# A new order for all engines, V of step 2 loaded earlier, and a third output tile in a fused attention and rational-MLP kernel

## The chip, the cores and the metric

The kernel runs on one core of a Trainium2 chip. The metric is the device time of one execution in microseconds (us); before the change the median of three runs is 232.0 us (231.14 to 232.74). Five engines work side by side, each through its own queue and strictly in the order written for it: TensorE (PE in the profile, its weight loads PEld), VectorE (DVE), ScalarE (ACT), GpSimd (POOL) and SyncE (SP). An instruction that waits on another engine or on a DMA holds up all that stands behind it in its own queue.

## The reference, cut to what matters

```python
# q, k, v: (4 batches, 8 heads, 768 positions, 64), float32
scores = q @ k.T / sqrt(64)
keep   = (pos_k < 4) | ((pos_q - pos_k >= 0) & (pos_q - pos_k < 128))   # 4 sink keys, window of 128
attn   = softmax(where(keep, scores, -1e9)) @ v
x      = attn.transpose(0, 2, 1, 3).reshape(3072, 512)
h      = x @ w_in                                   # 512 -> 2048
P      = a0 + a1*h + a2*h**2 + a3*h**3
Q      = 1 + |b0|*|h| + |b1|*h**2
out    = (P / (Q + 1e-6)) @ w_out                   # 2048 -> 512
```

## The kernel before, in words

The 3072 tokens are worked on in 12 steps of 256 tokens, three to a batch. A step s has an attention part and an MLP part; the attention runs some steps ahead of the MLP.

Attention of a step: K and Q are brought into the layout with the head dimension on the partitions. For the first four steps TensorE transposes them (`turn_k0`, `turn_q0`, `turn_kc`, `turn_qc`, line 661), and DVE or ACT copies the result out of PSUM (`place_k0`, `place_kc`, `place_qc`, the helper lines 677 on ACT and 679 on DVE). For later steps SyncE does it by a transposing DMA (lines 711, 715). V of the first three steps is loaded as rows (`load_vc`, line 474), sorted by TensorE (`turn_vc`, line 494) and placed (`place_vc`); later V goes straight to its place (`load_v`, line 465). `scores` (lines 761, 772, 786) come in four groups of a step, `exps` (ACT, line 805) takes the exponential, `attend` (line 846) multiplies by V, `rec` and `norm` (DVE, lines 854, 860) divide, `turn_x` (lines 880, 885) and `placed_x` give the transposed x of the MLP. The four sink keys of V are spread over the partitions by `cast_vs`, `turn_vs` and `spread_vs` (lines 533, 541, 555), in part 0 (batch 0) and part 1 (batches 1 to 3); `split_ab` (line 627) and `turn_vs:0` bring the coefficients a and b, which `norm` needs too.

MLP of a step m: `gemm1:m,j` (line 910, j from 0 to 3) multiplies by a quarter of w_in, `copy_in` (ACT, line 917) takes it out of PSUM, `sqa` (ACT) or `sqd` (DVE) squares it, `and`, `den`, `even`, `odd`, `odd_h`, `num`, `gate` (DVE, lines 930 to 964) are the rational function, `ln` and `exp` (ACT, lines 954, 959) the reciprocal of its denominator. `gemm2` (line 974) multiplies by w_out, `copy_out` and `store` bring out the rows. Steps 0 and 11 are cut into four parts for the elementwise work.

GpSimd issues the loads of w_in, w_out, V, K and Q (`load_kc` 440, `load_qc` 449, `load_k` 458, `load_q` 427, `load_w_in` 511, `load_w_out` 517), and holds some of them back by a one-element copy (`hold`, line 507) that waits for x_n or hb of a step.

Everything is cut into some 820 pieces. Each piece names its engine, its planned length, what it comes after, and, on TensorE, which of four PSUM tiles (`ps_h`, `ps_o`, `ps_m`, `ps_s`) it takes and which piece frees it. The list ORDER of numbers is the order in which the pieces are emitted, and so every engine's order; it comes from a search made ahead of time, and no planner runs in the kernel. ENGINE says for 32 copies whether DVE or ACT does them, BANK which PSUM tile each TensorE piece takes. A TensorE piece can start only when the piece that frees the last user of its tile is done. A negative number in ORDER is a stretch of idle matmuls (`spin`).

Of the kernel before, what the change touches and what calls it, by code (L numbers as in the profile page):

```python
# [65 lines left out]
def kernel(  # L66
# [54 lines left out]
    ENGINE = {('cast_q0', 1): 'DVE',  # L121
               ('place_kc', 3, None): 'DVE',
               ('place_qc', 0, 0): 'ACT',
               ('place_qc', 0, 1): 'ACT',
               ('k_sink', 0): 'DVE',
               ('place_qc', 1, None): 'DVE',
               ('place_qc', 2, None): 'DVE',
               ('place_qc', 3, 0): 'ACT',
               ('place_vc', 0): 'DVE',
               ('placed_x', 0, 0): 'ACT',  # L130
               ('placed_x', 0, 1): 'DVE',
# [8 lines left out]
               ('place_vc', 2): 'ACT',  # L140
               ('cast_k0', 0): 'DVE',
               ('place_k0', 0): 'DVE',
               ('cast_k0', 1): 'DVE',
               ('place_k0', 1): 'ACT',
               ('cast_q0', 0): 'ACT',
               ('place_kc', 1, None): 'ACT',
               ('place_kc', 2, None): 'ACT',
               ('place_qc', 3, 1): 'ACT',
               ('k_sink', 1): 'ACT',
# [23 lines left out]
             ('attend', 10, 0): 'ps_s',
             ('attend', 10, 1): 'ps_o',
             ('attend', 11, 0): 'ps_o',
             ('attend', 11, 1): 'ps_s',
             ('gemm1', 0, 0): 'ps_o',
             ('gemm1', 0, 1): 'ps_s',
             ('gemm1', 0, 2): 'ps_m',
             ('gemm1', 0, 3): 'ps_o',  # L180
             ('gemm1', 1, 0): 'ps_s',
             ('gemm1', 1, 1): 'ps_o',
# [14 lines left out]
             ('gemm1', 5, 0): 'ps_s',
             ('gemm1', 5, 1): 'ps_m',
             ('gemm1', 5, 2): 'ps_o',
             ('gemm1', 5, 3): 'ps_h',  # L200
# [13 lines left out]
             ('gemm1', 9, 1): 'ps_h',
             ('gemm1', 9, 2): 'ps_o',
             ('gemm1', 9, 3): 'ps_m',
             ('gemm1', 10, 0): 'ps_h',
# [1212 lines left out]
```

## Time and profile before

| | |
|---|---|
| median of 3 runs | 232.0 us (231.14 to 232.74) |
| the profiled execution: its time, its span | 232.42 us, 230.7 us |
| busy: TensorE, VectorE, ScalarE, GpSimd | 215.9, 211.1, 207.0, 97.3 us |
| granted TensorE clock over the span | 1.00 |

The profiled execution lies 0.4 us above the median; its time is 1.7 us longer than the span from its first to its last instruction. Three engines are busy for 90 to 94% of the span. In the slices of the page the idle part lies in the first 60 us and in the last 6.

### The profile page before, as it was taken

How to read it: one execution, taken by the hardware profiler on the slowest of the kernel's cores; microseconds unless marked ns; L12 is line 12 of the kernel's file. 1: busy time of each engine (PE TensorE's matmuls, PEld its weight loads, DVE VectorE, ACT ScalarE, POOL GpSimd, SP SyncE). 2: the span in 40 equal slices, each digit the busy share in tenths (PEclk: the TensorE clock that was granted, in tenths of full speed). 3: DMA queues.
4: the chain of work that ended last, by engine and by line, in shares of the span. 5: the costliest groups of instructions: out<-in, count | busy, mean ns of one | idle time of the engine just before them, and what ended most of it. 6: DMA issues, size and time to landing. Idle time of an engine off the chain costs nothing.

```text
span 230.7 us, 7350 instructions
## 1 busy us (share of the span) xinstructions
PE 215.9 (94%) x3249; PEld 147.0 (64%) x3271; DVE 211.1 (91%) x251; ACT 207.0 (90%) x177; POOL 97.3 (42%) x126
## 2 busy tenths in 40 slices
PE   8768999989999999999999999999999999999992
PEld 2546777778747667667677577758856875544441
DVE  3595699879999999999999999999999999999991
ACT  2757889989997999999999999999999999799961
POOL 8914756967559499988199800000000000000000
PEclk9999999999999999999999999999999999999999
DMA  6999999999999999999969998230050200400152
GB/s 182 199 191 199 197 144 103 135 117 121 205 176 141 130 106 150 172 122 124 196 155 133 109 148 162 47 71 0 3 139 3 48 0 0 182 4 0 49 224 91
DMA packets 95237, 26.98 MB, mean 117 GB/s; under 512 B 85862, under 2 KB 92262, under 8 KB 95206
## 3 DMA queue, kind: packets, MB, share of 16 engines
q0 software_dynamic: 65024, 12.98, 90.4%
q1 hardware_dynamic: 28942, 12.75, 29.8%
q10 hardware_dynamic: 1240, 0.79, 1.1%
q8 instruction: 25, 0.41, 0.8%
q14 instruction: 6, 0.05, 0.1%
HBM read 27.30 MB, written 6.29 MB: 146 GB/s over the span
## 4 chain that ended last, share of the span: by engine, by line
PE 69%; DMA 19%; POOL 3%; DVE 3%; issue 2%; ACT 2%; SPq 0%; DVEq 0%; ACTq 0%
PE ps_s L974 13%; PE ps_h L974 11%; PE ps_o L910 9%; PE ps_m L974 9%; PE ps_m L910 7%; DMA w_out_sb<-in_moe_w_out_dram 6%; PE ps_s L910 5%; PE ps_h L910 5%; DMA stage_v<-in_v_dram 4%; DMA k_bf<-in_k_dram 3%; DMA stage_a<-in_k_dram 2%; POOL v L465 2%; DMA ab_row<-in_moe_a_dram 2%; PE ps_o L846 2%; DMA q_bf<-in_q_dram 1%
## 5 line engine op out<-in xcount | busy, mean ns | idle before, releaser
L910 PEld LDWEIGHTS <-w_in_sb 128*128 128x128 bf16 x768 | 73.8, 98 | 13.0 <-issue 1.2
L974 PEld LDWEIGHTS <-g 128*128 128x128 bf16 x386 | 36.4, 98 | 41.6 <-issue 1.4
L954 ACT ACTIVATE lnq<-den 128x4096 f32<-128x4096 bf16 (+3 forms) x18 | 44.6, 2482 | 1.5 <-DVE den L935 1.4
L959 ACT ACTIVATE den<-lnq 128x4096 bf16<-128x4096 f32 (+3 forms) x18 | 44.5, 2484 | 0.2
L465 POOL DMA_DIRECT2D v<-in_v_dram x48 | 35.0, 746 | 3.6 <-DMA w_out_sb<-in_moe_w_out_dram 1.5
L910 PE MATMUL ps_o<-xblk,w_in_sb 128*128 128x256 bf16 x304 | 36.3, 273 | 0.0
L974 PE MATMUL ps_s<-w_out_sb,g 128*128 128x512 bf16 x136 | 32.3, 379 | 0.8 <-issue 0.5
L974 PE MATMUL ps_h<-w_out_sb,g 128*128 128x512 bf16 x121 | 28.6, 379 | 0.9 <-issue 0.5
L964 DVE TENSOR_TENSOR g<-num,den 128x4096 bf16<-128x4096 bf16 (+3 forms) x18 | 28.3, 1572 | 0.3
L935 DVE TENSOR_TENSOR den<-den,sq 128x4096 bf16<-128x4096 bf16 (+3 forms) x18 | 28.3, 1570 | 0.2
L951 DVE TENSOR_TENSOR num<-num,sq 128x4096 bf16<-128x4096 bf16 (+3 forms) x18 | 28.3, 1572 | 0.1
L948 DVE TENSOR_TENSOR sq<-sq,hb 128x4096 bf16<-128x4096 bf16 (+3 forms) x18 | 28.2, 1569 | 0.1
L910 PE MATMUL ps_m<-xblk,w_in_sb 128*128 128x256 bf16 x208 | 24.9, 273 | 0.5 <-DMA w_in_sb<-in_moe_w_in_dram 0.5
L974 PE MATMUL ps_m<-w_out_sb,g 128*128 128x512 bf16 x90 | 21.6, 379 | 0.6 <-issue 0.5
L917 ACT ACTIVATE hb<-ps_o 128x1024 bf16<-128x1024 f32 x19 | 19.5, 1029 | 2.1 <-PE ps_o L910 1.9
L924 ACT ACTIVATE sq<-hb 128x1024 bf16<-128x1024 bf16 (+3 forms) x15 | 20.0, 1341 | 0.1
L427 POOL DMA_DIRECT2D q_bf<-in_q_dram x15 | 16.7, 1111 | 6.0 <-DMA w_out_sb<-in_moe_w_out_dram 2.6
L910 PE MATMUL ps_s<-xblk,w_in_sb 128*128 128x256 bf16 x160 | 19.1, 273 | 0.0
L940 DVE TENSOR_SCALAR num<-sq,acoef 128x4096 bf16<-128x4096 bf16 (+3 forms) x18 | 18.3, 1023 | 0.3
L944 DVE TENSOR_SCALAR sq<-sq,acoef 128x4096 bf16<-128x4096 bf16 (+3 forms) x18 | 18.4, 1021 | 0.3
L507 POOL COPY seen<-x_n 1x1 bf16<-1x1 bf16 x8 | 9.7, 1225 | 17.4 <-DVE x_n L860 17.4
L926 DVE TENSOR_TENSOR sq<-hb 128x2048 bf16<-128x2048 bf16 (+2 forms) x13 | 16.8, 1295 | 0.1
(154 smaller groups left out, 321.5 us busy)
## 6 DMA issues: line engine op xcount, KB each, us to landing
out_dram<-o_t SPq DMA_DIRECT2D x11, 512.0 KB, 3.6
w_in_sb<-in_moe_w_in_dram POOLq DMA_DIRECT2D x4, 512.0 KB, 10.8
k_bf<-in_k_dram POOLq DMA_DIRECT2D x16, 128.0 KB, 6.6
w_out_sb<-in_moe_w_out_dram POOLq DMA_DIRECT2D x4, 512.0 KB, 11.7
q_bf<-in_q_dram POOLq DMA_DIRECT2D x15, 128.0 KB, 5.4
v<-in_v_dram POOLq DMA_DIRECT2D x24, 64.0 KB, 6.3
stage_v<-in_v_dram POOLq DMA_DIRECT2D x3, 256.0 KB, 9.6
v<-in_v_dram POOLq DMA_DIRECT2D x24, 32.0 KB, 5.7
```

The lines of the kernel that those rows point to most:

```text
L465: nc.gpsimd.dma_start(out=v_fix[b % 2][half(r), g * NHF:(g + steps) * NHF, hl, 0:D], in_=v[b, h, g * TS:(g + steps) * TS, :].rearrange("(j ...
L910: nc.tensor.matmul(ps[:, n, :], lhsT=w_in_all[:, c, fc * P:(fc + 1) * P], rhs=xblk[m][:, c, :], start=(c == 0), stop=(c == NDMC - 1))
L917: nc.scalar.activation(out=hb[m][:, j * GW:(j + 1) * GW], in_=ps_h.pop((m, j)).rearrange("p n c -> p (n c)"), func=AF.Copy)
L924: nc.scalar.activation(out=sq[m][:, c], in_=hb[m][:, c], func=AF.Square)
L935: nc.vector.tensor_tensor(out=den[m][:, c], in0=den[m][:, c], in1=sq[m][:, c], op=ALU.add)
L944: nc.vector.tensor_scalar(out=sq[m][:, c], in0=sq[m][:, c], scalar1=a3, scalar2=a1, op0=ALU.mult, op1=ALU.add)
L948: nc.vector.tensor_tensor(out=sq[m][:, c], in0=sq[m][:, c], in1=hb[m][:, c], op=ALU.mult)
L951: nc.vector.tensor_tensor(out=num[m][:, c], in0=num[m][:, c], in1=sq[m][:, c], op=ALU.add)
L954: nc.scalar.activation(out=lnq_fix[:, c], in_=den[m][:, c], func=AF.Ln, scale=qsc_reg, bias=1.000001)
L959: nc.scalar.activation(out=den[m][:, c], in_=lnq_fix[:, c], func=AF.Exp, scale=-1.0)
L964: nc.vector.tensor_tensor(out=g_of[m][:, c], in0=num[m][:, c], in1=den[m][:, c], op=ALU.mult)
L974: nc.tensor.matmul(ps_out[own][:, tt, cols], lhsT=g_of[m][:, co:co + P], rhs=w_out_all[:, fc, cols], start=(fc == 0), stop=(fc == NFFC - 1 ...
```

## The change

- ORDER is another permutation, ENGINE changes side for 20 of its 32 copies, BANK for most of the TensorE pieces.
- The first spin is 14 wide and 2 narrow matmuls in place of 13 and 2, and the second spin (5 matmuls, in step 0's attention) is gone.
- The pool of output tiles has three buffers, and `copy_out` of step m comes after `store` of step m-3 in place of m-2. To make room, the small tile `stage_s` (sink rows of V) becomes a slice of `stage_b`, which holds the first Q.
- `load_vc:2` moves on GpSimd's queue to the place right behind the first quarter of w_in.
- Nothing is computed in another way.

```diff
 ORDER = [
-    118, 2, 3, 0, -154, 108, 107, 129, 109, 117, 4, 119, 113, 116, 120, 121, 122, 1, 125, 143,
+    118, 2, 3, 0, -358, 108, 107, 109, 14, 119, 113, 120, 121, 122, 1, 116, 125, 5, 15, 8, 146,
...
-    ENGINE = {('cast_q0', 1): 'DVE',
-               ('place_kc', 3, None): 'DVE',
+    ENGINE = {('cast_q0', 1): 'ACT',
+               ('place_kc', 3, None): 'ACT',
...
-             ('scores', 0, 0): 'ps_h',
-             ('scores', 0, 1): 'ps_s',
+             ('scores', 0, 0): 'ps_o',
+             ('scores', 0, 1): 'ps_m',
...
-    o_sb = ctx.enter_context(tc.tile_pool(name="o_sb", bufs=2))
+    o_sb = ctx.enter_context(tc.tile_pool(name="o_sb", bufs=3))
...
-    stage_s = const_pool.tile([SR, B, D], FP32, name="stage_s")
+    stage_s = stage_b[0:SR, NQ0 * H * D:NQ0 * H * D + B * D].rearrange("p (b d) -> p b d", b=B)
...
-                      ends + [("store", m - 2, 0) if m >= 2 else None],
+                      ends + [("store", m - 3, 0) if m >= 3 else None],
...
-          [("gemm2", LAST, 1, parts(LAST) - 1), ("store", LAST - 2, 0)])
+          [("gemm2", LAST, 1, parts(LAST) - 1), ("store", LAST - 3, 0)])
```

Three places in the engines' queues follow, each first as it was and then as it is. Place one: GpSimd's loads around w_in (511 is w_in, 474 V rows of a step, 440 K rows, 449 Q rows, 458 K of later steps, 427 Q of later steps, 465 V of later steps). Before:

```order
L511 DMA w_in_sb<-in_moe_w_in_dram 128x4x512
L449 DMA stage_d<-in_q_dram 128x8x64
L511 DMA w_in_sb<-in_moe_w_in_dram 128x4x512 x2
L507 COPY seen<-x_n 1x1
L465 DMA v_92<-in_v_dram 64x4x64
L440 DMA stage_v<-in_k_dram 128x8x128
L511 DMA w_in_sb<-in_moe_w_in_dram 128x4x512
L474 DMA stage_v<-in_v_dram 128x8x128
```

Now:

```order
L449 DMA stage_d<-in_q_dram 128x8x64
L511 DMA w_in_sb<-in_moe_w_in_dram 128x4x512
L474 DMA stage_v<-in_v_dram 128x8x128
L511 DMA w_in_sb<-in_moe_w_in_dram 128x4x512 x2
L458 DMA k_bf<-in_k_dram 128x8x64
L511 DMA w_in_sb<-in_moe_w_in_dram 128x4x512
L427 DMA q_bf<-in_q_dram 128x8x64
L440 DMA stage_v<-in_k_dram 128x8x128
```

V of step 2 (474) has moved ahead of three quarters of w_in, K of step 3 (440) behind all four, and no hold copy stands among them.

Place two: DVE from `split_ab` on (627), with `spread_vs` (555, and 553 for the coefficients) in step 0's attention. Before:

```order
L627 TENSOR_TENSOR ab_part<-ab_row 1x8
L533 CAST sink_rows<-stage_s 32x192
L679 CAST v_91<-ps_o 128x16x64
L553 COPY ab_bc<-ps_m 128x8
L555 TENSOR_TENSOR v_sink<-ps_m,ind 128x8x64
L679 COPY qT_101<-ps_o 128x4x256
L745 TENSOR_TENSOR e_0_93<-e_0_93,sink_edge 128x4
```

Now:

```order
L627 TENSOR_TENSOR ab_part<-ab_row 1x8
L555 TENSOR_TENSOR v_sink<-ps_o,ind 128x8x64 x3
L553 COPY ab_bc<-ps_m 128x8
L555 TENSOR_TENSOR v_sink<-ps_m,ind 128x8x64
L634 SCALAR_TENSOR_TENSOR bpos<-ab_bc 128x3
L636 SCALAR_TENSOR_TENSOR bpos<-bpos 128x3
L745 TENSOR_TENSOR e_0_93<-e_0_93,sink_edge 128x4
```

The three rows of `spread_vs:1` came far later (behind the first `norm`) and now follow `split_ab` at once; they read `ps_o`, which by the new BANK is the tile that `scores:0,0` takes next.

Place three: GpSimd around w_out (517). Before:

```order
L465 DMA v_92<-in_v_dram 64x8x64 x5
L507 COPY seen<-x_n 1x1
L517 DMA w_out_sb<-in_moe_w_out_dram 128x4x512 x2
L465 DMA v_91<-in_v_dram 64x4x64
L517 DMA w_out_sb<-in_moe_w_out_dram 128x4x512 x2
```

Now:

```order
L465 DMA v_92<-in_v_dram 64x8x64 x7
L517 DMA w_out_sb<-in_moe_w_out_dram 128x4x512
L507 COPY seen<-x_n 1x1
L507 COPY seen<-hb 1x1
L517 DMA w_out_sb<-in_moe_w_out_dram 128x4x512
L427 DMA q_bf<-in_q_dram 128x8x64
L517 DMA w_out_sb<-in_moe_w_out_dram 128x4x512 x2
```

Between the first and the other three quarters of w_out there now stand two hold copies, `hold:x,3` (it waits for x_n of step 3) and `hold:h,1`.

## Rows read from the trace of the kernel before

**Rows 1.** The page: the span, and each engine's busy time and instructions.
```profile
span 230.7 us, 7350 instructions
PE 215.9 (94%) x3249; PEld 147.0 (64%) x3271; DVE 211.1 (91%) x251; ACT 207.0 (90%) x177; POOL 97.3 (42%) x126
```

**Rows 2.** Busy time by stretch: length, PE, PEld, DVE, ACT, POOL; clock, DMA share, GB/s.
```profile
0.00:28.79 28.79, 22.58 (x489) 15.38 (x491) 18.02 (x61) 18.84 (x23) 18.41 (x35) 1.00 1.36 194
28.79:57.85 29.06, 27.39 (x603) 22.72 (x598) 26.89 (x49) 26.93 (x32) 20.73 (x32) 1.00 2.22 124
...
60.00:220.00 160.00, 157.67 (x2054) 104.76 (x2075) 158.21 (x130) 155.11 (x116) 57.47 (x60) 1.00 1.07 99
220.00:230.70 10.70, 6.62 (x32) 2.82 (x31) 5.83 (x13) 4.00 (x7) 0.00 (x0) 1.00 0.37 139
```

**Rows 3.** Timeline, 10 to 30 us: start, length, engine, line, operation, idle before.
```profile
10.39 0.24 PE L761 MATMUL ps_h<-qT,k_sink 128*32 128x64 bf16 x8
...
11.10 0.15 DVE L627 TENSOR_TENSOR ab_part<-ab_row 1x8 bf16<-1x8 f32 x1 [1.48 <-DMA ab_row<-in_moe_a_dram]
...
11.36 0.18 PE L541 MATMUL ps_m<-sink_rows,spread 32*128 32x64 bf16 x1
...
14.07 1.22 DVE L679 COPY qT<-ps_o 128x1024 bf16<-128x1024 bf16 x1
...
15.96 0.21 DVE L854 RECIPROCAL rec<-ps_s 128x8 f32<-128x8 f32 x1
...
16.23 0.81 ACT L805 ACTIVATE e<-ps_m 128x768 bf16<-128x768 f32 x1 [0.69 <-PE ps_m L786]
...
17.67 1.89 DVE L555 TENSOR_TENSOR v_sink<-ps_o,ind 128x512 bf16<-128x512 f32 x3
...
19.70 0.75 DVE L860 SCALAR_TENSOR_TENSOR x_n<-ps_s,ratio,rec 128x512 bf16<-128x512 f32 x1
20.12 0.59 ACT L677 ACTIVATE xblk<-ps_o 128x512 bf16<-128x512 bf16 x1
...
20.51 0.40 PE L880 MATMUL ps_s<-ident,x_n 128*128 128x128 bf16 x4 [0.50 <-DVE x_n L860]
...
21.74 1.92 PE L910 MATMUL ps_o<-xblk,w_in_sb 128*128 128x256 bf16 x16
...
24.05 0.42 DVE L679 COPY qT<-ps_m 128x512 bf16<-128x512 bf16 x1 [2.67 <-PE ps_m L661]
...
25.31 1.06 ACT L924 ACTIVATE sq<-hb 128x1024 bf16<-128x1024 bf16 x1
...
26.86 0.68 DVE L935 TENSOR_TENSOR den<-den,sq 128x1024 bf16<-128x1024 bf16 x1
...
28.79 1.23 DVE L679 COPY kT<-ps_m 128x1024 bf16<-128x1024 bf16 x1 [0.23 <-PE ps_m L661]
```

**Rows 4.** Timeline of TensorE, 27 to 36 us.
```profile
27.97 0.77 PE L661 MATMUL ps_m<-ident,stage_v 128*64 128x128 bf16 x16 [0.45 <-DMA stage_v<-in_k_dram]
...
30.50 1.92 PE L910 MATMUL ps_m<-xblk,w_in_sb 128*128 128x256 bf16 x16 [0.53 <-DMA w_in_sb<-in_moe_w_in_dram]
...
32.48 1.91 PE L910 MATMUL ps_o<-xblk,w_in_sb 128*128 128x256 bf16 x16
```

**Rows 5.** The page's DMA issues: operation, count, KB each, median us to landing.
```profile
w_in_sb<-in_moe_w_in_dram POOLq DMA_DIRECT2D x4, 512.0 KB, 10.8
k_bf<-in_k_dram POOLq DMA_DIRECT2D x16, 128.0 KB, 6.6
```

**Rows 6.** Chain of waits: start, length, what; V rows of step 2.
```profile
22.99 9.62 DMA stage_v<-in_v_dram
```

**Rows 7.** Line 507, the hold copies: duration ns least, median, most; first and last start.
```profile
L507 POOL COPY seen<-x_n x8: 177/1284/2262, 20.5 to 114.7; 1x1 bf16<-1x1 bf16 x8
```

**Rows 8.** Timeline of TensorE, 56 to 70 us, the first products with w_out.
```profile
63.40 1.89 PE L974 MATMUL ps_h<-w_out_sb,g 128*128 128x512 bf16 x7
...
67.51 2.75 PE L974 MATMUL ps_h<-w_out_sb,g 128*128 128x512 bf16 x12 [0.27 <-DMA w_out_sb<-in_moe_w_out_dram]
```

More of the change, by code (lines that the diff above doesn't have):

```diff
@@ L120 @@
     PE_MASK = tuple(range(12))
-    ENGINE = {('cast_q0', 1): 'DVE',
-               ('place_kc', 3, None): 'DVE',
+    ENGINE = {('cast_q0', 1): 'ACT',
+               ('place_kc', 3, None): 'ACT',
                ('place_qc', 0, 0): 'ACT',
-               ('place_qc', 0, 1): 'ACT',
+               ('place_qc', 0, 1): 'DVE',
                ('k_sink', 0): 'DVE',
-               ('place_qc', 1, None): 'DVE',
-               ('place_qc', 2, None): 'DVE',
+               ('place_qc', 1, None): 'ACT',
+               ('place_qc', 2, None): 'ACT',
                ('place_qc', 3, 0): 'ACT',
-               ('place_vc', 0): 'DVE',
+               ('place_vc', 0): 'ACT',
                ('placed_x', 0, 0): 'ACT',
-               ('placed_x', 0, 1): 'DVE',
+               ('placed_x', 0, 1): 'ACT',
                ('placed_x', 1, 0): 'DVE',
@@ L137 @@
                ('placed_x', 4, 0): 'ACT',
-               ('placed_x', 4, 1): 'DVE',
+               ('placed_x', 4, 1): 'ACT',
                ('place_vc', 1): 'ACT',
[L140 to L149, printed above, removed]
+               ('place_vc', 2): 'DVE',
+               ('cast_k0', 0): 'ACT',
+               ('place_k0', 0): 'ACT',
+               ('cast_k0', 1): 'ACT',
+               ('place_k0', 1): 'DVE',
+               ('cast_q0', 0): 'DVE',
+               ('place_kc', 1, None): 'DVE',
+               ('place_kc', 2, None): 'DVE',
+               ('place_qc', 3, 1): 'DVE',
+               ('k_sink', 1): 'DVE',
                ('placed_x', 3, 0): 'DVE',
-               ('k_sink', 2): 'DVE',
-               ('k_sink', 3): 'ACT'}
-    BANK = {('attend', 0, 0): 'ps_s',
+               ('k_sink', 2): 'ACT',
+               ('k_sink', 3): 'DVE'}
+    BANK = {('attend', 0, 0): 'ps_h',
              ('attend', 0, 1): 'ps_s',
-             ('attend', 1, 0): 'ps_h',
-             ('attend', 1, 1): 'ps_s',
-             ('attend', 2, 0): 'ps_m',
+             ('attend', 1, 0): 'ps_o',
+             ('attend', 1, 1): 'ps_m',
+             ('attend', 2, 0): 'ps_h',
              ('attend', 2, 1): 'ps_h',
-             ('attend', 3, 0): 'ps_h',
-             ('attend', 3, 1): 'ps_m',
+             ('attend', 3, 0): 'ps_o',
+             ('attend', 3, 1): 'ps_h',
              ('attend', 4, 0): 'ps_m',
-             ('attend', 4, 1): 'ps_o',
-             ('attend', 5, 0): 'ps_m',
+             ('attend', 4, 1): 'ps_s',
+             ('attend', 5, 0): 'ps_h',
              ('attend', 5, 1): 'ps_h',
@@ L168 @@
              ('attend', 7, 1): 'ps_o',
-             ('attend', 8, 0): 'ps_s',
-             ('attend', 8, 1): 'ps_h',
+             ('attend', 8, 0): 'ps_o',
+             ('attend', 8, 1): 'ps_o',
              ('attend', 9, 0): 'ps_s',
              ('attend', 9, 1): 'ps_o',
[L173 to L182, printed above, removed]
+             ('attend', 10, 0): 'ps_o',
+             ('attend', 10, 1): 'ps_m',
+             ('attend', 11, 0): 'ps_h',
+             ('attend', 11, 1): 'ps_o',
+             ('gemm1', 0, 0): 'ps_m',
+             ('gemm1', 0, 1): 'ps_o',
+             ('gemm1', 0, 2): 'ps_o',
+             ('gemm1', 0, 3): 'ps_m',
+             ('gemm1', 1, 0): 'ps_m',
+             ('gemm1', 1, 1): 'ps_s',
              ('gemm1', 1, 2): 'ps_o',
-             ('gemm1', 1, 3): 'ps_m',
+             ('gemm1', 1, 3): 'ps_s',
              ('gemm1', 2, 0): 'ps_m',
-             ('gemm1', 2, 1): 'ps_o',
+             ('gemm1', 2, 1): 'ps_s',
              ('gemm1', 2, 2): 'ps_m',
              ('gemm1', 2, 3): 'ps_o',
-             ('gemm1', 3, 0): 'ps_o',
-             ('gemm1', 3, 1): 'ps_m',
-             ('gemm1', 3, 2): 'ps_s',
+             ('gemm1', 3, 0): 'ps_m',
+             ('gemm1', 3, 1): 'ps_o',
+             ('gemm1', 3, 2): 'ps_o',
              ('gemm1', 3, 3): 'ps_s',
-             ('gemm1', 4, 0): 'ps_o',
-             ('gemm1', 4, 1): 'ps_o',
+             ('gemm1', 4, 0): 'ps_m',
+             ('gemm1', 4, 1): 'ps_m',
              ('gemm1', 4, 2): 'ps_m',
              ('gemm1', 4, 3): 'ps_o',
[L197 to L200, printed above, removed]
+             ('gemm1', 5, 0): 'ps_h',
+             ('gemm1', 5, 1): 'ps_o',
+             ('gemm1', 5, 2): 'ps_m',
+             ('gemm1', 5, 3): 'ps_s',
              ('gemm1', 6, 0): 'ps_m',
-             ('gemm1', 6, 1): 'ps_o',
+             ('gemm1', 6, 1): 'ps_s',
              ('gemm1', 6, 2): 'ps_s',
@@ L206 @@
              ('gemm1', 7, 1): 'ps_m',
-             ('gemm1', 7, 2): 'ps_o',
+             ('gemm1', 7, 2): 'ps_m',
              ('gemm1', 7, 3): 'ps_s',
@@ L211 @@
              ('gemm1', 8, 2): 'ps_h',
-             ('gemm1', 8, 3): 'ps_m',
+             ('gemm1', 8, 3): 'ps_s',
              ('gemm1', 9, 0): 'ps_o',
[L214 to L217, printed above, removed]
+             ('gemm1', 9, 1): 'ps_s',
+             ('gemm1', 9, 2): 'ps_m',
+             ('gemm1', 9, 3): 'ps_h',
+             ('gemm1', 10, 0): 'ps_m',
              ('gemm1', 10, 1): 'ps_o',
-             ('gemm1', 10, 2): 'ps_s',
+             ('gemm1', 10, 2): 'ps_m',
              ('gemm1', 10, 3): 'ps_h',
@@ L256 @@
+             ('scores', 3, 3): 'ps_s',
+             ('scores', 4, 0): 'ps_m',
+             ('scores', 4, 1): 'ps_h',
              ('scores', 4, 2): 'ps_h',
              ('scores', 4, 3): 'ps_s',
-             ('scores', 5, 0): 'ps_h',
+             ('scores', 5, 0): 'ps_s',
              ('scores', 5, 1): 'ps_o',
-             ('scores', 5, 2): 'ps_o',
-             ('scores', 5, 3): 'ps_m',
-             ('scores', 6, 0): 'ps_m',
+             ('scores', 5, 2): 'ps_m',
+             ('scores', 5, 3): 'ps_o',
@@ L272 @@
+             ('scores', 8, 1): 'ps_o',
              ('scores', 8, 2): 'ps_m',
-             ('scores', 8, 3): 'ps_o',
-             ('scores', 9, 0): 'ps_s',
+             ('scores', 8, 3): 'ps_s',
+             ('scores', 9, 0): 'ps_h',
              ('scores', 9, 1): 'ps_s',
-             ('scores', 9, 2): 'ps_o',
-             ('scores', 9, 3): 'ps_o',
+             ('scores', 9, 2): 'ps_h',
+             ('scores', 9, 3): 'ps_h',
              ('scores', 10, 0): 'ps_s',
-             ('scores', 10, 1): 'ps_o',
+             ('scores', 10, 1): 'ps_m',
@@ L280 @@
              ('scores', 10, 2): 'ps_o',
-             ('scores', 10, 3): 'ps_m',
+             ('scores', 10, 3): 'ps_o',
              ('scores', 11, 0): 'ps_s',
              ('scores', 11, 1): 'ps_h',
-             ('scores', 11, 2): 'ps_h',
-             ('scores', 11, 3): 'ps_s',
-             ('turn_k0', 0): 'ps_m',
-             ('turn_k0', 1): 'ps_s',
-             ('turn_kc', 1, None): 'ps_h',
-             ('turn_kc', 2, None): 'ps_h',
-             ('turn_kc', 3, None): 'ps_m',
+             ('scores', 11, 2): 'ps_o',
@@ L291 @@
+             ('scores', 11, 3): 'ps_h',
+             ('turn_k0', 0): 'ps_s',
+             ('turn_k0', 1): 'ps_m',
+             ('turn_kc', 1, None): 'ps_o',
+             ('turn_kc', 2, None): 'ps_o',
+             ('turn_kc', 3, None): 'ps_h',
              ('turn_q0', 0): 'ps_h',
              ('turn_q0', 1): 'ps_o',
-             ('turn_qc', 1, None): 'ps_o',
-             ('turn_qc', 2, None): 'ps_m',
+             ('turn_qc', 1, None): 'ps_s',
+             ('turn_qc', 2, None): 'ps_s',
@@ L295 @@
              ('turn_qc', 3, 0): 'ps_m',
[L296 to L298 removed]
+             ('turn_qc', 3, 1): 'ps_s',
+             ('turn_vc', 0): 'ps_h',
+             ('turn_vc', 1): 'ps_m',
              ('turn_vc', 2): 'ps_s',
@@ L301 @@
              ('turn_vs', 1): 'ps_o',
-             ('turn_x', 0, 0): 'ps_o',
-             ('turn_x', 0, 1): 'ps_s',
-             ('turn_x', 1, 0): 'ps_h',
-             ('turn_x', 1, 1): 'ps_m',
-             ('turn_x', 2, 0): 'ps_m',
-             ('turn_x', 2, 1): 'ps_h',
-             ('turn_x', 3, 0): 'ps_s',
-             ('turn_x', 3, 1): 'ps_h',
-             ('turn_x', 4, 0): 'ps_m',
-             ('turn_x', 4, 1): 'ps_o'}
+             ('turn_x', 0, 0): 'ps_h',
+             ('turn_x', 0, 1): 'ps_o',
+             ('turn_x', 1, 0): 'ps_o',
+             ('turn_x', 1, 1): 'ps_s',
+             ('turn_x', 2, 0): 'ps_h',
+             ('turn_x', 2, 1): 'ps_o',
+             ('turn_x', 3, 0): 'ps_h',
+             ('turn_x', 3, 1): 'ps_o',
+             ('turn_x', 4, 0): 'ps_s',
+             ('turn_x', 4, 1): 'ps_m'}
     SQ_ACT = {2: 1, 4: 1, 6: 1, 8: 1, 10: 1}
```

40 lines of the change are left out of this document (17 added, 23 removed), and 82 rows, old and new, of the table ORDER.

## The prediction

> **What bounds the kernel now.** First the busy times of the whole span: TensorE 215.9, VectorE (DVE) 211.1, ScalarE (ACT) 207.0 of 230.7 us [rows 1]. No engine is far ahead, so a new order can win only where engines stand idle at the same time. The table by stretch says where. From 60 to 220 us DVE is busy 158.21 of 160, TensorE 157.67, ACT 155.11 [rows 2]: DVE has 1.8 us to give there, and every copy taken from it goes to an engine with 4.9 us free. From 28.79 to 57.85 DVE is busy 26.89 of 29.06 (2.2 idle). Up to 28.79 it is busy 18.02 and idle 10.8, and in the last 10.7 us it is busy 5.83; that end is a chain of the last step. Third the timeline of the start [rows 3]. It shows the 10.8 us to be a chain, not slack: data land, `split_ab` can start only at 11.10 when a and b have arrived (1.48 us idle before it), and 2.67 us of idle stand before the operation at 24.05. DVE's elementwise work needs the first `gemm1`, which starts at 21.74. So I read the kernel as one chain up to the first MLP quarter, and a nearly full DVE from then on: what counts is when DVE gets its elementwise work, and how much it has.
>
> The profiled execution took 232.42, that is 230.7 of span and 1.7 around it, and lies 0.4 above the median of 232.0. The sum is made on 232.42. About 1% (2.3 us) is what a measurement of this kernel can tell from no change.
>
> **The start, step by step.** Place two of the change decides here. `split_ab` still waits for the landing at 11.10, which nothing in the change touches; it ends near 12.0 with the small operations round it. Next on DVE is now `spread_vs:1`, 1.89 us [rows 3], so until 13.9. It frees the PSUM tile that `scores:0,0` takes, so these start at 13.9 where they started at 10.39. `scores:0,0` and `turn_vs:0` take 1.0 (10.39 to 11.36 in the old order): 14.9. `spread_vs:0` is a third of the 1.89 and a copy of 0.15, some 0.75: 15.65. Five small operations at about 0.15 (the size of `split_ab`) for the mask and coefficients: 16.4. `place_kc:1`, a 1024-column copy at 1.22: 17.6. `scores:1,3` and `attend:0,1`, between the 0.48 of two 0.24-us groups and the 1.89 that hid them before, taken as 0.9, being short: 18.5. `rec` 0.21 and two `norm` at 0.75, overlapping a little: 20.15. In the old order the second `norm` ended at 20.45, so to this point nothing is lost: what `spread_vs:1` costs early it no longer costs late.
>
> But one more copy stands ahead of the first MLP quarter. `place_kc:2` (was on ACT) is 1.22 on DVE: 21.3, and it frees the tile of `turn_x:0,1`, 0.40: 21.75. `placed_x` on ACT 0.59: 22.35. Before `exps:1,2` (0.81) stands `place_qc:2`, bounded by 0.42 for 512 columns on DVE and 0.81, taken as 0.6: 23.65 with both. `gemm1:0,0` takes the tile that these `exps` free, so it starts at 23.65, not 21.74: **1.9 us later**. w_in's first quarter is issued earlier than before and does not end this wait. DVE now idles from about 21.4 to 26.2, apart from step 1's `rec` and `norm`. `gemm1:0,0` (1.92), `copy_in` (near 1.0) and `sqa` (1.06) bring the squares at about 27.65; with `even` and the 12-block copy `place_qc:3,1` DVE reaches, at about 28.45, the place that `place_kc:3` had at 28.79.
>
> **What DVE then has to do.** Up to the point where step 1's wide `even` starts (57.85, the end of the second stretch [rows 2]) DVE had 26.89 of work after 28.79. Off it goes `place_kc:3`, 1.23 [rows 3], to ACT. On it come: `den` and `odd` of the first quarter, done before 28.79 in the old order, at most 0.68 each (1.3); `place_qc:3,1`, 768 columns, between the 0.42 for 512 and the 1.22 for 1024, taken as 0.9, near the middle; `place_vc:2` 1.22 less its overlap, 1.15; `k_sink:1`, taken as 0.3 (no more than 0.42). 26.89 - 1.15 + 1.3 + 0.9 + 1.15 + 0.3 = 29.4. From 28.45 that ends at 57.85, exactly where it ended before, if DVE never idles. It idled 2.17 there before; the new order has the same waits for `gemm1` and `attend`, and between 0 and 2.17 I take 0.5, because the extra copies are work that can fill gaps: 58.35. Of the later copies three 1024-column ones leave DVE and three come, one 512-column `placed_x` (0.42) leaves: -0.4. **Sum: 232.42 + 0.5 - 0.4 = 232.5**; less the 0.4 by which this execution stands above the median, about **232.0**, no change.
>
> **The loads around w_in** (place one). The four quarters of w_in are 512 KB each [rows 5]. The third quarter landed just ahead of `gemm1:0,2` at 30.50, and `turn_kc:3` started on its K at 27.97 [rows 4]: 512 KB in about 2.5 us, while the queue is full. V of step 2, issued last, landed at 22.99 + 9.62 = 32.61 [rows 6], 2.1 after that quarter and only 256 KB. With V moved ahead and K of step 3 behind all of w_in, K lands at 30.5 + 2.4 = 32.9 by the first rate and at about 34.5 by the second. `turn_kc:3` stands ahead of `gemm1:0,3` on TensorE, so that one goes to 34.0 from 32.48 (with 0.77 for `turn_kc:3` and the wait before it), 1.5 later; DVE has its own queue of three quarters' elementwise work meanwhile, and the sum holds no price for it. Its bounds are 0 and 2.5.
>
> **Costed at nothing.** The third output tile takes away a wait on a `store` that two steps earlier is long done in a saturated middle; `stage_s` inside `stage_b` changes an address. The first spin's one more 0.2-us matmul lies before the data land; the second one filled idle time at 16.6, and without it the granted clock, 1.00 in every stretch [rows 2], could fall, but TensorE has `attend`, transposes and scores around it. w_out (place three): its first quarter is needed at 63.40, and the second made TensorE wait 0.27 at 67.51 [rows 8]. Now `hold:x,3` and `hold:h,1` let the others go at about 55 and 58, to land near 61 to 68 by the 6.6 to 10.8 us of [rows 5], against first use at 63.6 and 70.2: covered, but by 2 us only.
>
> A hold copy of a single element took 177 to 2262 ns, half of them above 1284 [rows 7]: something holds GpSimd up while others work. If both holds and the three w_out issues behind them took 2.26 each, the last quarter would land at 73.8, not before 68, and TensorE would wait about 2.4. The Trainium skill, page "SBUF — State Buffer", section "SBUF: two separate sides", says that VectorE and GpSimd share a port pair which one of them holds for its whole instruction, and that this can keep GpSimd from writing DMA descriptors. By that rule the wide 4096-column DVE operations of step 1, which run at this very time, would hold the w_out issues up; the spread of [rows 7] agrees with it without proving it, and the sum would be 234.4 in place of 232.0.
>
> **Rivals.**
> (B) Faster. If the start's links are 0.6 shorter than I took them, the second stretch has no idle time, and the 1.8 idle between 60 and 220 goes too, the time is 232.0 - 0.6 - 0.5 - 1.8 = 229.1. For it: all three are small and the rows leave room for each. Against: DVE is at 98.9% in the middle, and nothing shown there is a wait that a new order must end. Chance 0.27.
> (C) Slower, from the start. K of step 3 lands at 34.5, `turn_kc:3` holds TensorE's queue, and `gemm1:0,3` and all of step 1's MLP come 2.5 to 3 late, at the same time as `gemm1:0,0` is 1.9 late. It decides once DVE has eaten its stock of elementwise work, by my count 1.5 to 2 us. Then 232.0 + 2.5 = 234.5. For it: both delays are read from rows. Against: DVE has some 5 us of quarter 0 to 2 to do from 28.45 on. Chance 0.15.
> (D) The w_out rival above: 234.4. Against: only if several issues in a row take the longest time of [rows 7]. Chance 0.06.
> (A) My forecast, 232.0, with 0.52; its own range is 230.2 to 233.8 (idle 0 to 2.17 in the second stretch, either way on the copies). That the change does nothing it says is inside it: the third tile gives nothing where no store is waited for.
>
> The range to hold 8 of 10 takes in most of B's way and C's own value: 229.0 to 234.8. Faster by over 1% (below 229.7): B, less what of it stays short, and a little of A, 0.26. Slower by over 1% (above 234.3): most of C and D, and the end of A, 0.19. Within: 0.55.
>
> **What would show it.** `scores:0,0` near 13.9; `gemm1:0,0` near 23.65; `turn_kc:3` at 33 and `gemm1:0,3` at 34; step 1's wide `even` on DVE near 58.3; DVE's idle time from 60 to 220 still near 1.8; no DMA wait at the second and third product with w_out; granted clock 1.00. I am wrong if `gemm1:0,0` starts before 22.5 or after 25, if DVE's wide `even` starts more than 1.5 away from 58.3, or if the middle's DVE idle time changes by over 1 us. If `turn_kc:3` starts after 35 with TensorE idle before it, it was C; if TensorE waits for w_out after 60, it was D.

## The result, and the profile after

The changed kernel takes 235.31 us (median of 4 runs, 235.04 to 235.49) beside 232.03 for the kernel before: the ratio is 1.0134, 95% interval 1.0106 to 1.0162, so **slower by 1.1 to 1.6%**. The forecast was 232.0 with a range that ended at 234.8. The ratios here and below leave out executions that ran over 1.5% longer than their kernel's fastest; the traces of r_after, e5_hold and a_shift48_k6 are of such executions. The profiled execution of the changed kernel has a span of 233.7 us, 3.0 more than [rows 1]. The page's first rows and the table by stretch, which answer to [rows 1, 2] (columns as there):

```profile
span 233.7 us, 7346 instructions
PE 215.1 (92%) x3243; PEld 146.6 (63%) x3267; DVE 211.4 (90%) x250; ACT 207.6 (89%) x178; POOL 96.4 (41%) x126
```

```profile
0.00:28.79 28.79, 22.00 (x473) 15.14 (x473) 17.09 (x56) 19.23 (x25) 18.98 (x34) 1.00 1.39 194
28.79:57.85 29.06, 25.60 (x574) 21.37 (x573) 26.12 (x51) 25.60 (x28) 17.39 (x27) 1.00 1.84 121
...
60.00:220.00 160.00, 155.82 (x2118) 104.19 (x2131) 157.48 (x127) 153.94 (x115) 57.87 (x64) 1.00 1.00 99
220.00:233.70 13.70, 9.55 (x45) 4.07 (x44) 8.65 (x17) 6.81 (x9) 0.00 (x0) 1.00 0.35 134
```

DVE has nearly the same work (211.4, before 211.1) and the clock is 1.00 throughout, so 2.7 of the 3.0 us are idle time of DVE. In the second stretch DVE idles 2.94 (2.17 before), from 60 to 220 it idles 2.52 (1.79). Two places account for it.

**Place one, at 37 us.** TensorE's timeline from 17 to 39 us (start, length, engine, line, operation, idle before and what ended it), rows that answer to [rows 4], with all stops of this kind:

```profile
17.72 0.19 PE L846 MATMUL ps_s<-v,e 64*64 64x65 bf16 x1 [0.58 <-issue]
...
30.18 0.28 PE L772 MATMUL ps_s<-qT,kT 64*64 64x192 bf16 x4 [0.82 <-issue]
...
31.14 1.92 PE L910 MATMUL ps_o<-xblk,w_in_sb 128*128 128x256 bf16 x16
...
33.55 0.64 PE L661 MATMUL ps_h<-ident,stage_v 128*64 128x128 bf16 x16
34.12 0.61 PE L910 MATMUL ps_m<-xblk,w_in_sb 128*128 128x256 bf16 x4
37.02 1.48 PE L910 MATMUL ps_m<-xblk,w_in_sb 128*128 128x256 bf16 x12 [2.28 <-issue]
38.34 0.39 PE L885 MATMUL ps_o<-ident,x_n 128*128 128x128 bf16 x4
```

`gemm1:0,3` is cut in two: 4 matmuls, 2.28 us of nothing, then 12. "Issue" says that the engine waited for nothing that the profile shows; the last quarter of w_in had landed at 30.8, K of step 3 at 33.17. Two smaller stops stand at 17.7 and 30.2. The kernel before has only two stops over 0.25 us up to 100 us, on the same timeline:

```profile
35.24 0.51 PE L494 MATMUL ps_s<-stage_v,sel 64*64 64x256 bf16 x10 [0.29 <-issue]
...
59.37 0.35 PE L846 MATMUL ps_m<-v,e 64*64 64x65 bf16 x19 [0.53 <-issue]
```

The stop costs DVE as much: its `placed_x` waits for the `turn_x` that stands behind `gemm1:0,3` (DVE's timeline, 36 to 60 us):

```profile
36.21 0.34 DVE L679 COPY k_sink<-kT 64x16 bf16<-64x16 bf16 x2
38.76 0.42 DVE L679 COPY xblk<-ps_o 128x512 bf16<-128x512 bf16 x1 [2.21 <-PE ps_o L885]
...
56.76 2.29 DVE L935 TENSOR_TENSOR den<-den,sq 128x4096 bf16<-128x4096 bf16 x1
...
59.83 1.34 DVE L940 TENSOR_SCALAR num<-sq,acoef 128x4096 bf16<-128x4096 bf16 x1
```

The last row is step 1's wide `even`: 59.83, where it was 57.85: 1.98 of the 3.0.

**Place two, at 90 us.** ACT waits for the sink keys of step 6, and DVE then waits for ACT (ACT's timeline, 82 to 92 us, here; DVE's below):

```profile
86.13 0.44 ACT L677 ACTIVATE k_sink<-kT 64x16 bf16<-64x16 bf16 x2 [2.41 <-DMA kT<-k_bf]
```

The rows of K of step 6 had landed at 34.0. What was late is the transposing DMA `turn_k:6,0`: on SyncE it stands behind `turn_q:14`, whose Q was issued at 63.70, behind the last quarter of w_out, and landed at 73.79 (SyncE's timeline, 60 to 92 us; the second `kT` of the last row is `turn_k:7,1`):

```profile
73.84 1.19 SPq L711 DMA_TRANSPOSE qT<-q_bf  x1
...
79.86 3.59 SPq L715 DMA_TRANSPOSE kT<-k_bf  x2
```

DVE's wait:

```profile
90.39 0.16 DVE L745 TENSOR_TENSOR e<-e,sink_edge 128x4 bf16<-128x4 bf16 x1 [1.40 <-ACT e L805]
```

From the wide `even` to the end it is 173.87 us, where it was 172.85: 1.02 more. DVE works 166.30 in it (166.16 before) and idles 7.57 (6.69): this wait of 1.40 is the cause, and 0.5 of other idle time has gone. So 1.98 + 1.02 = 3.0.

**What the stops are.** The page's row of the DMA queue that carries instructions, and the same row for 34.4 to 35.4 us alone (packets, MB, share of 16 engines):

```profile
q8 instruction: 25, 0.41, 0.8%
```

```profile
q8 instruction: 1, 0.02, 5.6%
```

25 packets of 16 KB over TensorE's 6,535 recorded instructions (6,559 in the traces of e3_k6 and a_wout, whose order of TensorE is the same). With its matmuls, weight loads and semaphore instructions counted in the order of their starts, the three stops have 449, 961 and 1217 instructions ahead of them, all of them 193 and a multiple of 256. The same count puts all 28 stops of this kind over 0.25 us from 5 to 100 us, in the traces of all 16 runs, at such a place. Such a packet moves for each 256 instructions, and its start can be set beside the time at which TensorE entered the block before (us, from the packets and starts of the traces):

```
kernel        block from  block before entered  packet          first instruction  stop
before        1217        28.50                 32.45 to 33.69  35.24              0.29
changed        961        24.07                 27.76 to 28.72  30.18              0.82
changed       1217        30.18                 34.49 to 35.38  37.01              2.28
e1_lean       1217        30.75                 31.80 to 33.04  35.03              none
a_hold_wout   1217        29.91                 32.08 to 32.97  34.58              0.3
```

In the first three rows, while loads fill the queues, a block comes 6.1 to 6.8 us after the block before was entered: some 4 us until the packet starts, 0.9 to 1.2 for it, 1.5 more. The time is about the same before and after the change; what differs is how soon TensorE has used up its 256 instructions. The packets have a queue of their own (q8 of the page, where GpSimd's loads are q0); by what the loads hold them up no row shows. Before, it took 6.2 us for them (the wait of 0.53 for w_in [rows 4] lay between); the new order took 4.3, and stood still for the rest.

### The profile page after: what moved, and what is told of

It reads as the page before. It is cut to its first block, busy times and chain, and to the rows that moved or that the text cites. A ratio compares the mean times of both kernels' runs of the same rounds, so it can differ in the third digit from the quotient of the medians.

```text
span 233.7 us, 7346 instructions
## 1 busy us (share of the span) xinstructions
PE 215.1 (92%) x3243; PEld 146.6 (63%) x3267; DVE 211.4 (90%) x250; ACT 207.6 (89%) x178; POOL 96.4 (41%) x126
## 5 line engine op out<-in xcount | busy, mean ns | idle before, releaser
L910 PEld LDWEIGHTS <-w_in_sb 128*128 128x128 bf16 x768 | 73.8, 98 | 15.9 <-issue 4.3
L910 PE MATMUL ps_m<-xblk,w_in_sb 128*128 128x256 bf16 x288 | 34.6, 273 | 2.6 <-issue 2.3
L974 PE MATMUL ps_h<-w_out_sb,g 128*128 128x512 bf16 (+1 forms) x136 | 32.7, 376 | 0.7 <-issue 0.3
L974 PE MATMUL ps_s<-w_out_sb,g 128*128 128x512 bf16 x121 | 28.9, 379 | 0.6 <-issue 0.3
L910 PE MATMUL ps_o<-xblk,w_in_sb 128*128 128x256 bf16 x208 | 24.9, 273 | 0.0
L910 PE MATMUL ps_s<-xblk,w_in_sb 128*128 128x256 bf16 x192 | 22.9, 273 | 0.1
L974 PE MATMUL ps_m<-w_out_sb,g 128*128 128x512 bf16 x89 | 21.0, 379 | 0.8 <-issue 0.6
L917 ACT ACTIVATE hb<-ps_m 128x1024 bf16<-128x1024 f32 x18 | 18.5, 1029 | 2.3 <-PE ps_m L910 1.5
L458 POOL DMA_DIRECT2D k_bf<-in_k_dram x16 | 16.3, 1018 | 7.6 <-DMA w_in_sb<-in_moe_w_in_dram 4.8
L427 POOL DMA_DIRECT2D q_bf<-in_q_dram x15 | 15.9, 1066 | 4.3 <-DMA w_out_sb<-in_moe_w_out_dram 1.6
```

Source lines behind the costliest of these rows:

```text
L910: nc.tensor.matmul(ps[:, n, :], lhsT=w_in_all[:, c, fc * P:(fc + 1) * P], rhs=xblk[m][:, c, :], start=(c == 0), stop=(c == NDMC - 1))
L917: nc.scalar.activation(out=hb[m][:, j * GW:(j + 1) * GW], in_=ps_h.pop((m, j)).rearrange("p n c -> p (n c)"), func=AF.Copy)
L974: nc.tensor.matmul(ps_out[own][:, tt, cols], lhsT=g_of[m][:, co:co + P], rhs=w_out_all[:, fc, cols], start=(fc == 0), stop=(fc == NFFC - 1 ...
```

## The experiments

Theory 1: TensorE runs out of instructions, whose packets are held up by the loads. Theory 2: the order of work and the data alone make the change slow. Times are compared by the ratio to the kernel before on the same chip (its median there was 232.3 to 232.9); the changed kernel itself (r_after) had 235.21 there, ratio 1.0106 (1.0064 to 1.0148). Line numbers shift a little from run to run: L908 and L912 below are `gemm1`, L910 above, and the others follow.

> The changed kernel itself, unedited, so that the runs beside it have it on the same chip: 234.9 to 235.7, with the stop of 2.3 us inside gemm1:0,3 again.

The stop stands behind the same fourth matmul in its trace, with 1.77 us in place of 2.28; in e3_k6 and a_wout below, with the same order of TensorE, it has 1.95 and 1.84. In these three `scores:0,0` starts at 13.73 to 13.77, 0.8 later than in the trace above, and the two smaller stops are at most 0.39.

**Emptier queue at 30 us (e1_lean).** GpSimd's pieces by name; `hold:x,1` moves up from 15 loads behind `load_kc:3`, and the four loads taken out ahead of it come behind it:

```diff
 load_w_in:2
-load_k:5,0
 load_w_in:3
-load_q:9
 load_kc:3
-load_k:6,0
-load_q:10
+hold:x,1
 load_v:3,7
...
-hold:x,1
```

> Edit: the changed kernel, but GpSimd waits for x_n of step 1 (hold:x,1) right behind K of step 3, and the loads of later K, Q and V come behind that wait, so the load queue runs empty at about 31 us. Theory 1 (TensorE's instructions arrive in blocks of 256, each fetched by a DMA that queues behind the loads; in the changed kernel the fetch of the block that begins 4 matmuls into gemm1:0,3 started 4.3 us after the block before it was entered, and TensorE stood still for 2.3 us at 34.7): that fetch starts 1 to 2 us after the block before it is entered in place of 4.3, the stop inside gemm1:0,3 shrinks from 2.3 to under 0.5 us, DVE's 2.2 us of idle at 38.8 goes, and the time falls from 235.3 to 232.5 to 233.8. Theory 2 (the stop is a wait for data, the last quarter of w_in or K of step 3, or the later start is simply the DVE work that I mis-counted): the stop stays, or moves by the 0 to 1 us by which those loads land earlier, and the time stays at 234.5 to 236.

237.59, ratio 1.0266 (1.0188 to 1.0344). The packet for block 1217 started after 1.05 in place of 4.30 and `gemm1:0,3` ran whole, so it is the loads under way that hold the packet up. The time missed its range: Q of step 4 was now late, and behind that wait the clock fell (TensorE's timeline, then the table by stretch, whose eighth figure is the granted clock):

```profile
34.69 1.92 PE L908 MATMUL ps_m<-xblk,w_in_sb 128*128 128x256 bf16 x16
...
51.27 0.24 PE L759 MATMUL ps_m<-qT,k_sink 128*32 128x128 bf16 x4 [2.56 <-DMA qT<-q_bf]
...
52.60 3.59 PE L908 MATMUL ps_s<-xblk,w_in_sb 128*128 128x256 bf16 x16
```

```profile
52.60:56.20 3.60, 3.60 (x27) 2.61 (x19) 3.60 (x6) 2.18 (x2) 2.30 (x4) 0.53 2.38 105
```

**Other block ends (e2_shift, a_shift128, a_shift256, a_shift48_k6, b_shift128).** Only idle matmuls at the very start differ (a_shift48_k6 also has the early `turn_k:6,0` of e3_k6, below), as here for 128 more instructions in the changed kernel; a matmul and its weight load are two:

```diff
-        for w in [wide] * (n // wide) + [1] * (n % wide):
+        for w in [wide] * 10 if at == 3 else [wide] * (n // wide) + [1] * (n % wide):
...
+        for w in [32] * 70 if at == 3 else []:
+            nc.tensor.matmul(cols[0:w, 0:w], lhsT=warm[:, 0:w], rhs=warm[:, 0:w], start=True, stop=True)
```

> Edit: the changed kernel, with the first stretch of idle matmuls cut into 2 wide and 46 narrow ones (14 wide and 2 narrow before), about as long, so that 64 more TensorE instructions stand ahead of everything else. Theory 1: the places where TensorE stops for its instructions move by 64 instructions toward the front of the program: the stop after the 4th matmul of gemm1:0,3 is gone, and one of 1 to 3 us stands 64 instructions earlier, in gemm1:0,2 or in the scores and attend ahead of it; the time stays within 1 us of 235.3, since the same number of fetches still has to pass the loaded queue. Theory 2: the stop stays behind the 4th matmul of gemm1:0,3, whatever stands ahead.

> Edit: the changed kernel with 128 more tiny TensorE instructions in its first idle stretch (10 wide and 70 of 32x32). Theory 1: the stop inside gemm1:0,3 is gone, others stand 128 instructions earlier, the largest before 25 us; by the same count they are 0 to 3 us longer in sum than in the changed kernel (3.7 before 40 us): 235.0 to 238. Theory 2: 234.7 to 235.6, the stop where it was.

> Edit: the changed kernel with 256 more TensorE instructions ahead of all work (4 wide idle matmuls and 140 of 32x32 in place of 14 and 2). Theory 1, blocks of exactly 256: one block more stands ahead, and every block end falls back on the same place in the work, so the stop stands again behind the 4th matmul of gemm1:0,3 with 1.5 to 2.5 us, and the time is the changed kernel's within 1 us (234.3 to 236.3). If the stops at other places after shifts of 64 and 128 came from the changed start and not from block ends, there is no reason for the stop to come back to this matmul.

64 more: 234.55, ratio 1.0109 (1.0063 to 1.0155); the stop is no longer in `gemm1:0,3` but 64 instructions earlier, in `turn_vc:2`. 128 more: 236.63, 1.0178 (1.0115 to 1.0241), with a start of TensorE's work 0.9 later, so only its places count. 256 more: 234.47, 1.0070 (1.0031 to 1.0109), and the stop is back behind the same fourth matmul. TensorE's timelines, 64, 128 and 256:

```profile
28.41 0.25 PE L770 MATMUL ps_h<-qT,kT 64*64 64x128 bf16 x4 [1.47 <-issue]
...
34.97 0.52 PE L492 MATMUL ps_s<-stage_v,sel 64*64 64x256 bf16 x12 [1.13 <-issue]
```

```profile
21.86 0.41 PE L661 MATMUL ps_s<-ident,stage_d 128*64 128x128 bf16 x7 [1.58 <-issue]
...
36.07 0.34 PE L848 MATMUL ps_m<-v,e 64*64 64x65 bf16 x12 [1.65 <-issue]
```

```profile
34.61 0.61 PE L912 MATMUL ps_m<-xblk,w_in_sb 128*128 128x256 bf16 x4
37.07 1.48 PE L912 MATMUL ps_m<-xblk,w_in_sb 128*128 128x256 bf16 x12 [1.85 <-issue]
```

Theory 2 has no reason for a stop that moves with idle matmuls and returns after 256. The kernel before, with 128 more (9 wide and 70 small in place of 13 and 2; its first transposes start 0.06 later):

> Edit: the kernel before the change, with its first stretch of idle matmuls cut into 9 wide ones and 70 of 32x32 (13 wide and 2 narrow before), so that 128 more TensorE instructions stand ahead of all work, in time in which TensorE waits for the first data anyway. Nothing else. Theory 1 (blocks of 256 instructions, each fetched behind the loads): the block ends fall 128 instructions earlier in the work, where TensorE eats 256 instructions faster (18 to 33 us: transposes, scores and attend of steps 0 to 2 with fewer products between); a count of the block ends against this kernel's own trace gives stops of 1.5 to 4 us between 18 and 36 us in place of 0.3, and the time rises by 1 to 4 us, to 233.3 to 236.3. Theory 2 (the change is slower because of its order of work and of data alone): idle matmuls ahead of the data change nothing, 231.5 to 232.9.

234.34, ratio 1.0067 (1.0030 to 1.0103): nothing but idle matmuls, and it loses 0.3 to 1.0%, with stops it did not have:

```profile
26.72 0.22 PE L848 MATMUL ps_h<-v,e 64*64 64x65 bf16 x2 [0.95 <-issue]
...
32.92 0.35 PE L848 MATMUL ps_s<-v,e 64*64 64x65 bf16 x18 [1.69 <-issue]
```

In this profiled execution the granted clock was also 0.57 from 14 to 18 us. Over all its executions the mean granted clock is 0.992, beside 0.991 for the kernel before on the same chip, so the clock is not what the 0.3 to 1.0% are.

> Edit: the changed kernel with 48 more TensorE instructions ahead (10 wide and 30 of 32x32), the count's best place for the block ends, and K of step 6 transposed early as in the third experiment. Theory 1: stops before 40 us 0.5 to 1 us shorter in sum, and no wait for step 6's sink keys: 232.8 to 234.0. Theory 2: as the third experiment, 233.8 to 234.4.

235.25, 1.0114 (1.0077 to 1.0151): a miss. The stops over 0.25 us before 40 us (0.33 and 1.83) sum to nearly as much as in e3_k6 (0.39 and 1.95); why it is also slower than e3_k6 stays open.

**The late K of step 6 (e3_k6, a_wout).** In e3_k6 on SyncE:

```diff
 turn_k:5,1
+turn_k:6,0
 turn_q:14
 turn_k:6,1
 turn_q:13
 turn_q:12
-turn_k:6,0
```

> Edit: the changed kernel, with SyncE's transposing DMA for the first half of K of step 6 (turn_k:6,0, its rows landed at 34) moved from behind turn_q:12, where it started at 79.9, to behind turn_k:5,1 at about 49. Theory: ACT's copy of step 6's sink keys no longer waits 2.4 us at 83.7, the exponentials of step 6 are earlier, DVE's only large idle time after 60 us (1.4 us at 90.4) goes, and the time falls by 0.9 to 1.4 us to 233.9 to 234.4. Rival (DVE is held elsewhere right behind it, or the wait at 90.4 is hidden): 235.0 to 235.5.

234.10, 1.0065 (1.0038 to 1.0093), as expected: the sink keys are copied at 84.07 with no wait (ACT's timeline, 80 to 90 us):

```profile
84.07 0.45 ACT L675 ACTIVATE k_sink<-kT 64x16 bf16<-64x16 bf16 x2
```

In a_wout on GpSimd:

```diff
 load_w_out:0
-hold:x,3
-hold:h,1
 load_w_out:1
 load_q:12
 load_w_out:2
 load_w_out:3
+hold:x,3
+hold:h,1
```

> Edit: the changed kernel with its two hold copies for x_n of step 3 and hb of step 1 moved on GpSimd behind the last quarter of w_out, so that quarters 2 to 4 of w_out and the loads behind them are issued from 52 us on in place of 59. If the late loads behind these holds are what makes K of step 6 late (and so the 2.4 us wait of ACT and the 1.4 us of DVE at 90): that wait shrinks under 0.7 us and the time falls by 0.7 to 1.4 us to 233.9 to 234.6. If the order of SyncE's transposes alone makes it late: the wait stays, 235.0 to 235.6. A fuller queue at 52 to 60 us can also delay the TensorE block entered at 53.5: then a stop of up to 1 us shows at 60.

233.96, 1.0067 (1.0034 to 1.0099): quarters 2 to 4 of w_out are issued 6 to 7 us earlier and the Q of `turn_q:14` behind them 3.9 earlier, `turn_k:6,0` starts at 75.1 in place of 79.9, and the wait is gone. So the two hold copies of place three are what made K of step 6 late. How long the wait is differs between traces: ACT's is 0.37 in e2_shift and 0.99 in a_shift256, which have the changed kernel's orders for GpSimd and SyncE.

**Both together (e4_both, e5_hold, e6_hold_k6, a_hold_wout).** e5_hold waits for an earlier signal than e1_lean, with the pieces' order to match:

```diff
-        t_ = x_n[s][0:1, 1, 0:1] if kind == "x" else hb[s][0:1, MW - 1:MW]
+        t_ = x_n[s][0:1, int(s != 1), 0:1] if kind == "x" else hb[s][0:1, MW - 1:MW]
```

> Edit: the first and the third together on the changed kernel. If both losses are independent they add: 231.2 to 232.8, level with the kernel before the change (232.0). If the later one only follows from the earlier one (a late start makes late loads and a late K of step 6), then this is no faster than the first alone.

> Edit: the changed kernel; GpSimd's hold behind K of step 3 now waits for the first half of x_n of step 1 (ready at 26.8, 6 us before the whole), K and Q of steps 4 and 5 come behind it, and K of step 6 and one V load for it behind the V loads of step 3. So the queue runs low at about 30 us, as in the first experiment, but the loads held back are issued by 41 us as in the changed kernel. Theory 1: the fetch of the block entered at about 30.2 starts after 1 to 2 us in place of 4.3, the stop inside gemm1:0,3 is under 0.5 us, and this time no scores of step 4 wait for a late Q; step 1's wide even on DVE starts at 57.8 to 58.8 (59.83 in the changed kernel, 63.1 in the first experiment), and the time is 233.0 to 234.2. Theory 2 (what made the first experiment slower is not the late Q but the altered load order itself, and the stop costs nothing): 235 or more.

> Edit: the hold of the experiment before, and the transposing DMA for K of step 6 moved ahead as in the third experiment. If the two losses are independent and are all that the change lost: 231.8 to 233.0. If the second only follows from the first: as the hold alone, 233.0 to 234.2.

e4_both: 238.62, 1.0271 (1.0212 to 1.0329), as slow as e1_lean. e5_hold: 234.02, 1.0049 (1.0026 to 1.0072). e6_hold_k6: 234.00, 1.0048 (1.0015 to 1.0081), no more than the hold alone or e3_k6 alone, and a miss. The stop in `gemm1:0,3` fell to 0.49, but TensorE, earlier now, ran out of instructions again at 52, among the V loads of step 4 and w_out, and step 1's wide `even` starts at 59.86, no earlier than in the changed kernel (e6_hold_k6, TensorE):

```profile
35.08 1.49 PE L910 MATMUL ps_m<-xblk,w_in_sb 128*128 128x256 bf16 x12 [0.49 <-issue]
...
53.51 1.14 PE L910 MATMUL ps_m<-xblk,w_in_sb 128*128 128x256 bf16 x9 [1.58 <-issue]
```

So the gain of e5_hold over the changed kernel is not shown to come from the shorter stop; its one trace, where no wait for step 6's sink keys is left, does not tell. a_hold_wout takes the hold of e5_hold and the moved holds of a_wout:

> Edit: the changed kernel with the early hold behind K of step 3 (as in the fifth experiment) and with its two late hold copies behind the last quarter of w_out (as in the eleventh). What is open: in the fifth and sixth experiments the stop inside gemm1:0,3 shrank and the DVE ran 1.4 us earlier at 45 us, but a new stop of 1.6 us stood at 53. If the time now is 232.4 to 233.4, the two remedies add and the stops and the late loads account for what the change lost; if it is 233.5 to 234.5 (like either alone), the stop at 53 gives the first remedy's gain back.

232.67, **ratio 1.0010 (0.9977 to 1.0042)**: the two remedies undo the whole loss. Of the stop in `gemm1:0,3` some 0.3 us is left (it takes 2.22 in place of 1.92), and no other over 0.16 up to 100 us. DVE's timeline at step 1's wide `even`, and the table by stretch:

```profile
58.31 1.34 DVE L940 TENSOR_SCALAR num<-sq,acoef 128x4096 bf16<-128x4096 bf16 x1
```

```profile
60.00:220.00 160.00, 157.75 (x2053) 104.53 (x2075) 158.87 (x131) 155.33 (x117) 51.25 (x60) 1.00 0.98 97
```

From `scores:0,0` to the `even` it is 45.21 us here and 46.63 in a_wout, which lacks only the early hold and has the stop of 1.84. Why there is no new stop at 52 stays open: that packet started 0.66 after the block before was entered, in e6_hold_k6 2.88. The kernel is level with the one before, not faster; no run here beat that one by more than its interval.

**The reverse (e7_unheld).** In the kernel before, `hold:x,0` goes behind `load_k:4,1`, eight loads later.

> Edit: the kernel before the change, with its hold copy for x_n of step 0 (GpSimd waits there from 12.7 to 20.5 us) moved behind a K load of step 4, so that its loads are issued without a pause, as in the changed kernel; nothing else. Theory 1 (a full load queue delays TensorE's instruction blocks): the fetches of the blocks entered at 23.9 and 28.5 start 3.3 to 4.4 us after (2.3 and 4.0 before), TensorE stops for 1 to 2 us in all between 25 and 37, and the time rises by 0.4 to 1.8 us to 232.6 to 234.0, though K of step 3 and the third quarter of w_in land earlier. Theory 2 (the queue does not matter, data do): those two earlier landings take away 0.45 and 0.53 us of waits, and the time is 231.4 to 232.2.

232.62, 0.9990 (0.9963 to 1.0016): a miss for the expected starts, and no test of the theory. The packets for the blocks from 961 and 1217 started after 2.40 and 2.32, not 3.3 to 4.4, so the loads were not in their way, and in the profiled execution the granted clock was 0.62 to 0.68 from 14 to 24 us, which started `gemm1:0,0` 2.0 late.

## Why the prediction was wrong, point by point

- **The step that failed** is the one on the loads around w_in: that `gemm1:0,3` goes to 34.0, that "DVE has its own queue of three quarters' elementwise work meanwhile", and that "the sum holds no price for it", with bounds 0 and 2.5. The loads were read rightly: `turn_kc:3` started at 33.55 and `gemm1:0,3` at 34.12. But TensorE's own instructions were held up by the same loads: the stop of 2.28 us inside `gemm1:0,3`, behind which DVE had nothing to do for 2.21. No term of the sum held that. It cost 1.5: `even` at 59.83 against 58.35 in the working, 1.53 from the 58.3 where the prediction drew its line at 1.5, and at 58.31 once the stops were removed (a_hold_wout). The row with 0.29 "issue" in the trace before was there to be read; that the cost lies inside the bounds of 0 and 2.5 is luck, for the cause is another.
- **w_out** was half right. TensorE never waited for it, as the sum has it, but its quarters landed at 60.3, 64.7, 70.4 and 72.9, as in rival D and not in the 61 to 68 of the sum. The price was paid by what is queued behind: Q of `turn_q:14`, then K of step 6 behind it on SyncE, and so ACT's 2.41 and DVE's 1.40. The working asked who waits for w_out alone.
- In **rival D's** place the hold behaved as its rows said: `hold:x,3` took 2.78 us (GpSimd's timeline):

```profile
56.31 2.78 POOL L507 COPY seen<-x_n 1x1 bf16<-1x1 bf16 x1 [3.81 <-DVE x_n L860]
```

  It ended at 59.09, and the 4096-column DVE operation that started at 56.76 ended at 59.05. The Trainium skill, page "SBUF — State Buffer", section "SBUF: two separate sides", says that a DVE operation with two SBUF inputs and a GpSimd operation that reads SBUF lock each other out for a whole instruction. This pair of rows agrees so far as the copy ended when the DVE operation did.
- **The start** came out right, in part by luck. `scores:0,0` began at 12.95 (13.9 in the working; a and b landed 0.9 earlier in this execution) and `gemm1:0,0` at 23.19 (23.65). Between the two it is 10.24, where the working has 9.75, and 10.65 in e3_k6, where a and b landed at 10.97; the early landing hid that:

```profile
12.95 0.24 PE L761 MATMUL ps_o<-qT,k_sink 128*32 128x64 bf16 x8 [0.70 <-DVE v_sink L555]
...
23.19 1.91 PE L910 MATMUL ps_m<-xblk,w_in_sb 128*128 128x256 bf16 x16 [0.22 <-ACT e L805]
```

- **DVE's work** was mis-sized twice, with opposite signs: from `place_qc:3,1` (28.08) to the wide `even` it is 28.70 (29.4 in the working), and behind it 0.14 more than before (0.4 less in the working). Its idle time up to the `even` is 3.05, where I took 0.5; 2.21 of it is the one wait behind the stop. The sum, which holds neither the stop nor the late K, says no change, and a_hold_wout, which is rid of both, measures level with the kernel before; that the two sizes cancel is luck.
- **Slips of the sum:** 22.35 with 0.6 and 0.81 is 23.76, not 23.65, and 232.42 + 0.5 - 0.4 - 0.4 is 232.1; how the last quarter of w_out comes to 73.8 is not worked out. None of them changes the forecast.
- **Costed at nothing:** the granted clock stayed 1.00 without the second spin in this execution. In that of a_hold_wout it was 0.69 from 14 to 18 us, and in that of b_shift128, which keeps the spin, 0.57: what the spin is worth stays open, but a_hold_wout is level even so. The third output tile was not tried alone, since the new order puts four stores behind the `copy_out` that two tiles would make wait for them.
- **Rival C** named the place, not the mechanism: K of step 3 landed at 33.17, and no wait for it shows.
